# First loads of a gated mix kernel: x tile 0 split over two DMA queues by partitions, the other x tiles from SyncE, the Wk chunks but one from ScalarE

## The chip, the cores and the metric

One core of a Trainium2 chip runs the kernel. The metric is the device time of one execution in microseconds (us). Each kernel was run several times and profiled; a profile's times count from the first instruction of the span, which is about 2 us shorter than the device time. Engines are PE (TensorE's matmuls), PEld (its weight loads), DVE (VectorE), ACT (ScalarE), POOL (GpSimd) and SP (SyncE). SPq and ACTq are the instructions with which SyncE and ScalarE issue transfers on their DMA queues.

## The reference, cut to what matters

The output mixes two branches over one input x of 2048 x 512 elements in bf16: linear attention with 32 heads, and a layernorm with an MLP over tokens, gated by a sigmoid.

```python
qkv = x @ wqkv                         # D = 512, Wk is columns 512 to 1023
phi = lambda t: where(t > 0, t + 1, exp(t)) + 1e-6
kv  = einsum("bhsd,bhse->bhde", phi(k), v)
...
return g * a + (1 - g) * b
```

Only the start matters here: the first product is k = x @ Wk. It needs x transposed, tile by tile (a tile is 128 rows of x, 128 KB), and Wk in four chunks of 128 rows (128 KB each, `wk0` to `wk3`).

## The kernel before

The first eight loads go out on two queues in turn. The tiles x0 to x3 are transposed on PE; later tiles are transposed by the DMA. Six dummy matmuls on a constant (`warm_up`) keep PE busy until x0 lands.

```python
load_x(nc.sync, 0, 1)          # load_x(queue, first tile, tiles)
load_x(nc.scalar, 1, 1)
load_wk(nc.sync, 0)
load_x(nc.scalar, 2, 1)
load_x(nc.sync, 3, 1)
for k, q in ((1, nc.scalar), (2, nc.sync), (3, nc.scalar)):
    load_wk(q, k)
load_xT(4, 2)                  # DMA transposes, from SyncE
...
warm_up(6)
...
transpose_tile(0, False)       # four 128x128 transposes on PE, then a copy to xT
transpose_tile(1, True)
transpose_tile(2, False)
...
for k in range(2):             # six kacc matmuls: tiles 0 to 2, chunks wk0, wk1
    for t in range(HEADS - 1):
        k_part(t, (k,))
transpose_tile(HEADS - 1, True)
...
for t in range(HEADS):         # 14 kacc matmuls: the rest of tiles 0 to 3
    k_part(t, range(2 if t < HEADS - 1 else 0, ND))
    k_phi(t)
# ... (then kacc of tile t and gacc of tile t - 4 in turn, and all other stages)
```

PE takes its instructions in this order, so the transposes of x1 wait for x1 even when something later could run.

## Time and profile before

| | before |
|---|---|
| device time, median (lowest to highest of 4 runs) | 165.77 us (165.58 to 165.94) |
| span of the profiled run | 163.6 us |
| PE busy | 159.9 us, 98% |
| first `kacc` matmul starts | 4.82 us |
| first `gacc` matmul starts | 9.85 us |

These lines of the page of the kernel before give the span, each engine's busy time, PE's busy tenths in 40 slices, and the chain that ended last:

```profile
span 163.6 us, 2078 instructions
...
PE 159.9 (98%) x785; PEld 73.6 (45%) x785; DVE 87.8 (54%) x200; ACT 58.7 (36%) x90; POOL 18.3 (11%) x37
...
PE   7999999999999999999999999999999999999993
...
PE 98%; DVE 0%; issue 0%
```

PE is the limit from the first slice to the last, so a microsecond that PE loses anywhere is a microsecond of the kernel.

The chain view of the kernel before, for the first 14 us (start, duration, what):

```profile
0.84 2.72 PE wps L108 x6
3.56 1.47 PE pt L194 x12
5.03 1.74 PE kacc L108 x6
6.77 0.22 PE pt L194 x4
6.99 3.02 PE kacc L108 x14
10.01 0.86 PE gacc L108 x4
```

`wps` are the warm-ups, `pt` the transposes. Six warm-ups take 2.72 us, about 0.43 us each in steps of start to start. Fourteen later `kacc` matmuls of the same size take 3.02 us, 0.216 us each: PE starts at half speed. In the trace the steps change between 5.25 and 5.96 us.

The waits of the first 14 us, and the first two issues of SyncE in the timeline (start, duration):

```profile
PEld L194 <- DMA xs<-in_A_x_dram: 1.0, 2, 0.8
```

```profile
0.81 0.40 SPq L124 DMA_DIRECT2D xs<-in_A_x_dram  x1
1.27 0.41 SPq L127 DMA_DIRECT2D wk_sb<-in_A_wqkv_dram  x1
```

The weight loads of the transposes wait 1.0 us in two waits. The longer one, 0.75 us, passes while PE still works on the warm-ups.

### The profile page before, as it was taken

Reading aid. Unit: us, or ns where it says so; the run is one execution under the profiler, and the core shown is the slowest. Engines: PE = TensorE matmul, PEld = TensorE weight load, DVE = VectorE, ACT = ScalarE, POOL = GpSimd, SP = SyncE. Lnnn points to the kernel's source line nnn. Section 1 sums busy time; section 2 is a strip of 40 time slices with the busy share of each in tenths; the row PEclk is TensorE's granted clock in tenths of the full one; section 3 lists DMA queues with packets and bytes.
Section 4 is the critical chain, followed back from the end, with each engine's and each line's share of the span. In section 5 each row is a group of like instructions: output and inputs, shape, how many; then the busy total and the mean of one; then the engine's idle time right before and its main releaser. Section 6 shows DMA issues by size and latency. Waiting matters only on the chain.

```text
span 163.6 us, 2078 instructions
## 1 busy us (share of the span) xinstructions
PE 159.9 (98%) x785; PEld 73.6 (45%) x785; DVE 87.8 (54%) x200; ACT 58.7 (36%) x90; POOL 18.3 (11%) x37
## 2 busy tenths in 40 slices
PE   7999999999999999999999999999999999999993
PEld 3444444444544444434444444444444444444452
DVE  0599999958999999109995301156221111111112
ACT  3463386658478373311332113111112222211110
POOL 5000710200200000001055500050000000000000
DMA  5999999999930005800993499932010000111001
GB/s 152 242 243 236 294 300 344 349 348 348 317 78 0 0 0 188 264 0 0 277 303 109 149 289 307 337 126 98 32 36 32 32 32 32 42 50 41 32 32 32
DMA packets 30057, 25.05 MB, mean 153 GB/s; under 512 B 7968, under 2 KB 29472, under 8 KB 30048
## 3 DMA queue, kind: packets, MB, share of 16 engines
q1 hardware_dynamic: 28032, 22.02, 45.5%
q0 software_dynamic: 1440, 2.38, 5.4%
q10 hardware_dynamic: 576, 0.52, 1.1%
q8 instruction: 6, 0.10, 0.2%
q14 instruction: 3, 0.02, 0.0%
HBM read 21.11 MB, written 2.23 MB: 143 GB/s over the span
## 4 chain that ended last, share of the span: by engine, by line
PE 98%; DVE 0%; issue 0%
PE uacc L108 30%; PE yps L108 30%; PE kacc L108 9%; PE aps L108 8%; PE qacc L108 8%; PE gacc L108 8%; PE wps L108 2%; PE pt L194 1%; PE denps L108 1%; PE kvps L108 1%; DVE ot L474 0%; PE zps L108 0%; PE pt L323 0%
## 5 line engine op out<-in xcount | busy, mean ns | idle before, releaser
L108 PE MATMUL uacc<-hs,w1c 128*128 128x512 bf16 x224 | 52.1, 379 | 0.0
L108 PE MATMUL yps<-uT,w2c 128*128 128x512 bf16 (+2 forms) x238 | 51.0, 366 | 0.0
L474 DVE SCALAR_TENSOR_TENSOR ot<-yps,c,a_sc 128x512 bf16<-128x512 f32 (+2 forms) x17 | 12.2, 720 | 45.9 <-PE yps L108 45.8
L108 PEld LDWEIGHTS <-w2c 128*128 128x128 bf16 x238 | 22.8, 98 | 25.9
L108 PEld LDWEIGHTS <-w1c 128*128 128x128 bf16 x224 | 21.7, 98 | 26.0 <-issue 0.4
L461 ACT ACTIVATE a_sc<-aps,c,gg 128x512 f32<-128x512 f32 x16 | 12.4, 778 | 46.7 <-PE aps L108 43.0
L317 ACT ACTIVATE uT<-uacc,bcol 128x512 bf16<-128x512 f32 x14 | 9.3, 687 | 27.7 <-PE uacc L108 27.7
L108 PE MATMUL aps<-W2sb,pqT 128*128 128x512 bf16 x64 | 16.4, 379 | 0.0
L108 PE MATMUL qacc<-xT,wq_sb 128*128 128x512 bf16 x64 | 16.4, 379 | 0.0
L108 PE MATMUL kacc<-wk_sb,xT 128*128 128x512 bf16 x64 | 16.4, 385 | 0.0
L108 PE MATMUL gacc<-pk,xs 128*128 128x512 bf16 x64 | 15.8, 379 | 0.0
L244 ACT ACTIVATE hs<-xs,nmr,rstd 128x512 bf16<-128x512 bf16 x16 | 12.8, 805 | 1.9 <-DVE nmr L238 1.9
L204 ACT ACTIVATE e<-qacc 128x512 bf16<-128x512 f32 x16 | 9.6, 597 | 10.1 <-PE qacc L108 9.2
L413 POOL DMA_DIRECT2D rex<-rd_dram x16 | 9.5, 603 | 23.0 <-DVE pqT L415 18.2
L204 ACT ACTIVATE e<-kacc 128x512 bf16<-128x512 f32 x16 | 9.3, 595 | 6.9 <-PE kacc L108 6.8
L208 DVE SCALAR_TENSOR_TENSOR pk<-kacc,e 128x512 bf16<-128x512 f32 x16 | 11.1, 692 | 0.6
L208 DVE SCALAR_TENSOR_TENSOR pqT<-qacc,e 128x512 bf16<-128x512 f32 x16 | 11.1, 692 | 0.6
L228 DVE BATCH_NORM_STATS2 stats<-xs 128x6 f32<-128x512 bf16 x16 | 10.9, 682 | 0.0
L205 DVE TENSOR_SCALAR e<-e 128x512 bf16<-128x512 bf16 x32 | 9.0, 282 | 3.3 <-ACT e L204 3.3
L400 DVE CUSTOM_DVE_ANT_0 junk<-xs,gw_b 128x512 bf16<-128x512 bf16 x16 | 9.8, 685 | 0.0
L269 DVE TENSOR_TENSOR zacc<-zacc,pk 128x512 f32<-128x512 f32 x14 | 9.6, 686 | 0.2
L108 PEld LDWEIGHTS <-wq_sb 128*128 128x128 bf16 x64 | 6.3, 98 | 7.5
(64 smaller groups left out, 70.1 us busy)
## 6 DMA issues: line engine op xcount, KB each, us to landing
w2c<-in_B_w_dram SPq DMA_DIRECT2D x8, 896.0 KB, 7.5
w1c<-in_B_w_dram SPq DMA_DIRECT2D x2, 2048.0 KB, 15.5
w1c<-in_B_w_dram SPq DMA_DIRECT2D x3, 1024.0 KB, 12.3
rex<-rd_dram POOLq DMA_DIRECT2D x16, 128.0 KB, 2.9
out_dram<-ot SPq DMA_DIRECT2D x15, 128.0 KB, 1.7
xs<-in_A_x_dram SPq DMA_DIRECT2D x3, 512.0 KB, 4.5
wq_sb<-in_A_wqkv_dram SPq DMA_DIRECT2D x1, 512.0 KB, 6.8
wv_sb<-in_A_wqkv_dram SPq DMA_DIRECT2D x1, 512.0 KB, 12.3
```

Of the source, the lines that this page charges most:

```text
L108: nc.tensor.matmul(o, lhsT=lhsT, rhs=rhs, start=start, stop=stop, **kw)
L204: nc.scalar.activation(out=e[:], in_=acc[:], func=ACT.Exp)
L205: nc.vector.tensor_scalar(out=e[:], in0=e[:], scalar1=1.0, scalar2=PHI_EPS, op0=ALU.min, op1=ALU.add)
L208: nc.vector.scalar_tensor_tensor(out=dst, in0=acc[:], scalar=0.0, in1=e[:], op0=ALU.max, op1=ALU.add)
L228: nc.vector.bn_stats(out=stats[:], in_=xs[:, t, :])
L244: nc.scalar.activation(out=hs[:, t, :], in_=xs[:, t, :], func=ACT.Identity, scale=rstd[:, t : t + 1], bias=nmr[:, t : t + 1],)
L269: nc.vector.tensor_tensor(out=zacc[:], in0=first, in1=pk[:, t, :], op=ALU.add)
L317: nc.scalar.activation(out=uT[:, j, :], in_=acc[:], func=ACT.Gelu_apprx_tanh, bias=bcol[:, j : j + 1])
L400: nc.vector.tensor_tensor_reduce(out=junk[:], in0=xs[:, t, :], in1=gw_b[:], scale=1.0, scalar=0.0, op0=ALU.mult, op1=ALU.add, accum_out=gp ...
L413: nc.gpsimd.dma_start(out=rex[:], in_=src.unsqueeze(1).to_broadcast([8, HEAD, SC]))
L461: nc.scalar.activation(out=a_sc[:], in_=aps[:], func=ACT.Identity, scale=gg[:, t : t + 1], bias=c2[:, t : t + 1],)
L474: nc.vector.scalar_tensor_tensor(out=ot[:, :W], in0=yps[:, :W], scalar=c1[:, t : t + 1], in1=a_sc[:, cs], op0=ALU.mult, op1=ALU.add,)
```

## The change

The intent, as the code shows it: get x0 sooner by carrying half of it on each queue, take out the warm-up that is then not needed, and keep the x tiles on one queue and the Wk chunks (all but wk2) on the other. Merging the first w2 load's halves takes back the transfer that the split adds, so the later loads reuse the same completion semaphores.

```diff
-    load_x(nc.sync, 0, 1)
-    load_x(nc.scalar, 1, 1)
-    load_wk(nc.sync, 0)
-    load_x(nc.scalar, 2, 1)
+    for q, p in ((nc.sync, slice(0, P // 2)), (nc.scalar, slice(P // 2, P))):
+        q.dma_start(out=xs[p, 0, :], in_=x_view[p, 0, :])
+    load_x(nc.sync, 1, 1)
+    load_wk(nc.scalar, 0)
+    load_x(nc.sync, 2, 1)
+    load_wk(nc.scalar, 1)
     load_x(nc.sync, 3, 1)
-    for k, q in ((1, nc.scalar), (2, nc.sync), (3, nc.scalar)):
-        load_wk(q, k)
+    load_wk(nc.scalar, 3)
+    load_wk(nc.sync, 2)
...
-    warm_up(6)
+    warm_up(5)
...
-        for f0 in (0, NF // 2):
-            f1 = f0 + NF // 2
+        for f0, f1 in ((0, NF // 2), (NF // 2, NF)) if c else ((0, NF),):
```

## The prediction

> **What bounds the kernel now.** TensorE. The page gives PE 98% busy (159.9 of 163.6 us), and the chain of waits is 98% PE. The change touches only the first 7 us of it: six warm-up matmuls (2.72 us), twelve x-tile transposes (1.47), six `kacc` matmuls (1.74), four transposes, then `kacc` back to back. Here PE waits for data only twice: in the waits view the transposes' weight loads wait 1.0 us for x tiles (0.75 us before 3.41, behind the warm-ups, and 0.24 us before 4.42). The limits are the arrival of x tiles 0 to 2 and the slow clock: in the timeline matmuls start 0.42 us apart until about 5.7 us and 0.216 us after it.
>
> **What the change moves.** No arithmetic. One 0.43 us warm-up goes, one issue (about 0.42 us of a sequencer) comes on SyncE; merging the first w2 load's halves takes one back near 60 us, where PE never waits for it.
>
> Before, issue to landing was: x0 0.81 to 3.4, x1 0.80 to 3.5, wk0 1.27 to 4.2, x2 (second on ACT) to 4.4, x3 1.73 to 5.7, wk1 to 5.9, wk2 to 6.5, wk3 to 6.8. Both queues moved bytes at like rates (DMA view by window), 290 to 350 GB/s together. The Trainium skill, "DMA: Bandwidth & Descriptors", Rules for kernel authors, calls splitting a transfer into partition halves pointless, since both use the same 16 engines; the trace agrees that the queues share. What the split changes is order: both queues first carry half of x0, so x0 no longer competes with x1. From packets moved per window I estimate
>
> - x0: 3.4 -> 3.2 us (ACT's half decides; its first packets came about 0.25 us after SP's)
> - x1: 3.5 -> 3.7
> - x2: 4.4 -> 4.6 (third on SP, behind 64 + 128 KB, not second on ACT behind 128 KB)
> - wk0, wk1: near 4.0 and 5.4, before PE needs them
> - x3 6.0, wk3 6.3, wk2 6.7.
>
> wk2 is now the ninth load: the compiled order makes SyncE wait for x0's first half before issuing it, because eight completion semaphores are reused in turn; before, the first DMA transpose had that wait (0.9 us). Its issue goes from 2.2 to about 3.1 us, but the rings are still full then.
>
> **On the critical path.** Warm-ups end near 2.98; transposes 0 start near 3.2 instead of 3.42, but transposes 2 near 4.6 instead of 4.42, so `kacc` starts 0.2 us later; half of that is slow-clock time, so it costs about 0.1 us. If x2 lands as before, the gain is likewise halved: removing 0.43 us of slow-clock warm-up saves at most about 0.2 us. I predict 165.6 us, range 165.1 to 166.4; faster by over 2% 0.01, within 2% 0.97, slower 0.02.
>
> **What would show it.** x0's transposes start at 3.0 to 3.3 us; the wait ahead of x2's grows from 0.24 to 0.3 to 0.6; first `kacc` 4.8 to 5.2; the `kacc` block before transpose 3 ends at 6.5 to 7.0; after that all stages keep their lengths, shifted by a constant. No PE wait for wk1, wk2, wk3 or w2c.
>
> **What would make it wrong.** (1) The clock. The Trainium skill, "TensorE: Matmul & The Clock Gate", Part 1, says that full clock needs a busy window of about 3.4 us; the trace agrees with a slow start. The change leaves about 0.8 us of PE idle there instead of about 0.2; if this delays the fast clock by a window, it costs up to 1.7 us: about 167.3. I give that 10 to 15%. (2) wk2 landing after 7.0 us stalls PE at full clock. (3) x2 landing as early as before: 165.3.

## The result, and the profile after

| | before | after |
|---|---|---|
| device time, median (lowest to highest of 4 runs) | 165.77 us (165.58 to 165.94) | 168.56 us (168.07 to 168.72) |
| ratio | | 1.0163, 95% interval 1.0144 to 1.0183 |
| span of the profiled run | 163.6 us | 166.8 us |
| x0, x1, x2 landed | 3.37, 3.54, 4.38 us | 3.23, 4.90, 6.11 us |
| first `kacc` matmul starts | 4.82 us | 6.38 us |
| first `gacc` matmul starts | 9.85 us | 12.86 us |

A ratio is the mean time of one kernel's runs over the mean of the other's of the same rounds, so it is not quite the ratio of the medians quoted. Landing times are the trace's start of issue plus its time to landing. The kernel is 2.8 us slower, and the time lies outside the predicted range of 165.1 to 166.4.

The same lines of the page after the change, with one more: this page has a row of the granted clock (PEclk, in tenths), which the page before did not print.

```profile
span 166.8 us, 2064 instructions
...
PE 160.1 (96%) x770; PEld 73.6 (44%) x784; DVE 87.8 (53%) x200; ACT 59.0 (35%) x90; POOL 18.2 (11%) x37
...
PE   6599999999999999999999999999999999999992
...
PEclk9879999999999999999999999999999999999999
...
PE 94%; DMA 2%; SPq 1%; issue 1%; DVE 0%
```

PE's busy time is nearly the same, but the first two slices (8 us) have gaps, and the second and third slices have a lower clock (8 and 7). The chain view of the changed kernel for the first 14 us:

```profile
0.80 0.58 SPq L135
...
1.44 0.82 SPq L124
...
2.31 3.79 DMA xs<-in_A_x_dram
...
6.15 0.41 PE pt L196 x4
...
6.59 0.43 DVE xT L202
...
7.07 1.68 PE kacc L108 x4
8.74 0.43 PE pt L196 x4
9.17 3.86 PE kacc L108 x14
13.03 0.86 PE gacc L108 x4
```

Up to 6.1 us the chain no longer runs through PE but through SyncE's issues and the transfer of x2. Behind it the same 14 `kacc` matmuls take 3.86 us instead of 3.02. From `gacc` on everything is shifted: the first `gacc` block starts at 13.03 in this chain against 10.01, 3.02 us later, and the first `yps` block at 102.46 against 99.44, also 3.02. So 3.02 of the 3.2 us between the two profiled spans arose before 13 us.

The waits of the first 14 us of the changed kernel:

```profile
PEld L196 <- DMA xs<-in_A_x_dram: 3.3, 3, 1.3
...
PE pt L196 <- DMA xs<-in_A_x_dram: 2.0, 3, 1.0
```

PE itself now stands still for x tiles, 2.0 us in three waits; before, only its weight loads had to wait. The granted clock shows what that does. Two windows of the changed kernel (columns: stretch, its length, busy time of PE, PEld, DVE, ACT and POOL with instructions, granted clock, DMA share, GB/s):

```profile
3.90:7.32 3.42, 1.53 (x13) 0.70 (x13) 1.16 (x3) 1.17 (x3) 0.00 (x0) 1.00 1.08 282
7.32:10.73 3.41, 3.41 (x13) 1.49 (x12) 1.27 (x5) 1.19 (x2) 0.00 (x0) 0.50 1.08 242
```

The trace's record of the clock has exactly these edges: full from 3.90 to 7.32 us, half from 7.32 to 10.73, full from there on. The full clock came early in this run, fell on a stretch in which PE was busy for 1.53 of 3.42 us, and was taken away for the next 3.41 us, when the data was there.

Only one of the four runs of the changed kernel shows this loss. Half clock for 3.41 of 166.8 us gives a mean granted clock of 0.99, as the profiled run has it; the other three have 1.0, and took 168.07 to 168.62 us all the same. In the traces at hand the clock record begins only with the first full clock, so a full clock that came late would fit these three (the order run below has that form); but no trace of them is on record, and this is not shown.

This gives a first sum for the profiled runs. The first `kacc` starts 1.56 us later (6.38 against 4.82). From there to the first `gacc` it takes 6.48 instead of 5.03 us, 1.45 more: 0.25 us of it is a wait for x2's copy, the rest slow clock.

The issues on SyncE's queue in the changed kernel's timeline:

```profile
0.80 0.58 SPq L135 DMA_DIRECT2D xs<-in_A_x_dram  x1
1.44 0.82 SPq L124 DMA_DIRECT2D xs<-in_A_x_dram  x1
```

The issue of 64 partitions took 0.58 us, not 0.40, and the whole tile behind it 0.82, not 0.41. The DMA view from 2.75 to 3.25 us, before the change (q1 is SyncE's queue, q10 ScalarE's; packets, MB, share of the engines),

```profile
q1 hardware_dynamic: 117, 0.11, 69.5%
q10 hardware_dynamic: 87, 0.07, 42.6%
```

and after it:

```profile
q10 hardware_dynamic: 90, 0.09, 91.6%
q1 hardware_dynamic: 15, 0.01, 16.5%
```

SyncE's queue, which now carries x1 and x2, nearly ran dry at the time when it should have moved x1.

### The profile page after: what moved, and what is told of

Same layout as the page of the kernel before. It is cut to its first block, busy times and chain, and to the rows that moved or that the text cites. A ratio compares the mean times of both kernels' runs of the same rounds, so it can differ in the third digit from the quotient of the medians.

```text
span 166.8 us, 2064 instructions
## 1 busy us (share of the span) xinstructions
PE 160.1 (96%) x770; PEld 73.6 (44%) x784; DVE 87.8 (53%) x200; ACT 59.0 (35%) x90; POOL 18.2 (11%) x37
## 4 chain that ended last, share of the span: by engine, by line
PE 94%; DMA 2%; SPq 1%; issue 1%; DVE 0%
PE yps L108 29%; PE uacc L108 29%; PE kacc L108 9%; PE qacc L108 8%; PE aps L108 8%; PE gacc L108 8%; DMA xs<-in_A_x_dram 2%; PE denps L108 1%; PE kvps L108 1%; PE wps L108 1%; PE pt L196 1%; SPq L124 0%; SPq L135 0%; DVE xT L202 0%; DVE ot L475 0%
## 5 line engine op out<-in xcount | busy, mean ns | idle before, releaser
L108 PE MATMUL kacc<-wk_sb,xT 128*128 128x512 bf16 x64 | 17.6, 407 | 0.1
L108 PEld LDWEIGHTS <-xT 128*128 128x128 bf16 x64 | 6.5, 104 | 8.2 <-issue 1.4
```

Of the source, the lines that this page charges most:

```text
L108: nc.tensor.matmul(o, lhsT=lhsT, rhs=rhs, start=start, stop=stop, **kw)
```

## The experiments

Three questions stood after the result. Is the order of the loads or the split to blame? Is the loss the late data alone, or also the clock? And what decides when a tile lands? There were twelve runs, one of them a repetition; all gave correct results. "Before" in each group is the kernel before, run on the same chip in the same rounds. Landing times differ by up to 0.9 us between runs of the same loads (x2 came at 4.70 to 5.61 us in the three profiles with the partition split alone), so they are quoted run by run, each from its own profile.

### The order without the split

```diff
+    load_x(nc.sync, 0, 1)      # whole, from SyncE
+    load_x(nc.sync, 1, 1)
+    load_wk(nc.scalar, 0)      # and on as in the changed kernel; warm_up(5)
```

> The changed kernel without the split: x0 whole on SyncE, then x1, x2, x3, wk2 there, wk0, wk1, wk3 on ScalarE's queue, five warm-ups, w2 load as before. Theory Order (x1 and x2 come late because they stand in line behind x0 on one queue while wk chunks, which nobody needs yet, take half of the bandwidth): x1 lands at 4.2 to 4.9 us, x2 near 5.7 to 6.1, full clock after 9 us, time 168.0 to 168.6. Rival Split (the half-tile issues, 0.58 us instead of 0.40, and the slow issue behind them, 0.82 us, make everything late): every issue takes 0.40 to 0.45 us, x1 and x2 land by 4.0 and 5.0, time below 166.8.

Measured: 168.5 us (167.13 to 168.69; before 165.65), ratio 1.0158, interval 1.0112 to 1.0205. SyncE's issues took 0.40 to 0.43 us. x1 landed at 4.16 us, x2 at 5.79, and the record of the full clock starts at 9.44. The chain of this run:

```profile
1.73 4.06 DMA xs<-in_A_x_dram
...
5.84 0.61 PE pt L195 x4
6.45 2.56 PE kacc L108 x6
```

Six `kacc` matmuls in 2.56 us are all at half speed. What follows: the order alone, with five warm-ups, costs as much as the whole change within the intervals (one of its four runs took only 167.13). Theory Order stands for the sum; the split is not needed for it.

### The split without the order

```diff
-    load_x(nc.sync, 0, 1)
+    for q, p in ((nc.sync, slice(0, P // 2)), (nc.scalar, slice(P // 2, P))):
+        q.dma_start(out=xs[p, 0, :], in_=x_view[p, 0, :])
```

> The kernel before, with x0 alone split in two; the rest of the order, six warm-ups and the w2 load as before (x1 and x2 now second and third on ScalarE's queue). Theory Order: the split by itself costs x1 and x2 at most half a tile of queueing, x1 lands by 4.0 and x2 by 5.0; PE idles less than 0.8 us, full clock near 5.7 us, 165.6 to 166.2. Rival Split: issues of 0.55 us and more and a slow issue after each half, x1 not before 4.5, x2 not before 5.5, full clock after 9 us, 167.5 to 168.6.

Measured: 166.74 us (166.35 to 168.77), ratio 1.0107, interval 1.0033 to 1.0181. Both theories missed. x1 landed at 3.81, x2 at 5.27 and the clock was full from 4.76: the median lies between the two expectations. Because of the outlier the same kernel was run again:

> The partition split alone once more (same kernel as e2_split_only, on another chip or at another time), because its four runs ran from 166.35 to 168.77. x2 third on ScalarE's queue at 4.7 to 5.3 us. If the split alone costs about 1 us as the median said: median 166.4 to 167.0, with some runs above 167.5 where the clock came late. If it costs nothing and that median was chance: 165.6 to 166.1.

Measured: 166.5 us (166.23 to 168.07; before 165.8), ratio 1.006, interval 1.0026 to 1.0094; x2 landed at 5.61, later than I had expected. The split alone costs something near 0.6 to 1.1%. One caveat: in this kernel ScalarE issues five loads instead of four, and its function-table load starts at 3.48 us instead of 2.70; part of the cost may lie there, which was not tested.

### The split by columns

```diff
+    for q, c in ((nc.sync, slice(0, D // 2)), (nc.scalar, slice(D // 2, D))):
+        q.dma_start(out=xs[:, 0, c], in_=x_view[:, 0, c])
```

> The kernel before with x0 split over the two queues by columns (128 partitions times 256 elements each) instead of by partitions (64 times 512); the rest as in the kernel before, so it stands against the run with the partition split alone (issues 0.58 and 0.56 us, the next SyncE issue 0.82, x2's transposes at 5.32). Theory Form (a transfer of 64 partitions is slow to issue): both column halves issue in 0.40 to 0.46 us, the next SyncE issue too; x2's transposes start before 4.9; 165.6 to 166.2. Rival Queue (any second transfer ahead of x1 and x2 costs this, whatever its form): x2's transposes after 5.1, 166.4 to 167.0.

Measured: 166.55 us (166.34 to 168.24; before 165.89), ratio 1.0058, interval 1.0007 to 1.0109. The timeline has SyncE's issues as:

```profile
0.81 0.40 SPq L135 DMA_DIRECT2D xs<-in_A_x_dram  x1
1.27 0.43 SPq L127 DMA_DIRECT2D wk_sb<-in_A_wqkv_dram  x1
```

So it is the form of 64 partitions that issues slowly, not half a tile of bytes; that part of Theory Form is right. x2 landed at 4.75, and x0 at 2.97, 0.40 sooner than in the kernel before. But the six warm-ups kept PE until 3.36, so the early x0 was not used (columns with fewer warm-ups were not run), and the time did not come down to what I expected: here PE waited for wk1, which landed at 6.32 (behind three transfers on ScalarE's queue). In time the two kinds of split cannot be told apart. Why 64 partitions issue slowly stays open.

### The changed kernel with dummy matmuls in its gaps

```diff
-    warm_up(5)
+    warm_up(6)
     transpose_tile(0, False)
+    warm_up(3)
     transpose_tile(1, True)
+    warm_up(2)
```

> The changed kernel with six warm-ups and five more dummy matmuls (three after x0's transposes, two after x1's), so that PE has work while it waits for x1 and x2. Theory Clock (most of the loss is that the idle time kept the clock slow): full clock near 5.7 us again though x1 and x2 land as late as in the changed kernel; kacc then starts near 6.6 at full clock; 166.8 to 167.3. Rival Lateness alone (the clock comes up late for some other reason, or the loss is the wait itself): full clock still after 9 us, 168.3 or more.

Measured: 167.07 us (166.53 to 167.13), ratio 1.0082, interval 1.0054 to 1.0111, half of the change's loss. The same two windows as above, in this run:

```profile
3.90:7.32 3.42, 3.33 (x21) 1.56 (x19) 1.69 (x5) 1.18 (x3) 0.00 (x0) 1.00 1.09 288
7.32:10.73 3.41, 3.41 (x21) 1.68 (x19) 2.45 (x6) 2.66 (x5) 0.00 (x0) 1.00 1.26 239
```

More work for PE went with a faster kernel, and the clock, full from 4.75 us, stayed full. The time is what theory Clock expected. The profile was kinder than I had assumed, though: it is of the fastest of the four runs, and x2 landed at 5.33 us in it, not at 6.1, so this run by itself does not separate the two causes cleanly. The next one does.

### The order alone with dummy matmuls

```diff
     transpose_tile(1, True)
+    warm_up(3)                 # on the order without the split; warm_up(6) at the start
```

> The changed order without the split (the earlier run took 168.5, full clock from 9.4 us), now with six warm-ups and three dummy matmuls between x1's and x2's transposes, where PE waited 1.0 us. Theory Clock: the arrivals stay (x1 near 4.2, x2 near 5.8) but the clock is full by 6.5 and stays so, 166.5 to 167.2. Rival Lateness: the wait for x2 is the loss, 168.2 or more.

Measured: 167.18 us (167.13 to 167.37; before 165.89), ratio 1.0073, interval 1.0056 to 1.009, against 1.0158 without the dummies. x2 landed at 6.16 us, 0.37 later than in the profile without them, and still the kernel was faster. This chain answers to the one above:

```profile
1.75 4.41 DMA xs<-in_A_x_dram
...
6.21 0.41 PE pt L195 x4
...
7.12 1.04 PE kacc L108 x4
```

Four `kacc` matmuls in 1.04 us are at full speed; the clock was full from 3.66 us. So about half of the loss of the order goes away when PE has work in the gaps: that is the clock's part. The other half, some 0.7%, stays with the late data. The halves are rough, since the clock in this profile was full even earlier than in the kernel before (3.66 us against some time from 5.25 to 5.96).

### The split alone with dummy matmuls

```diff
     transpose_tile(1, True)
+    warm_up(2)                 # on the split without the order
```

> The partition split alone (earlier run 166.35 to 168.77, x2's transposes at 5.32), with two dummy matmuls between x1's and x2's transposes. If the run of 168.77 was one in which the clock came late or was lost, all four runs now lie within 166.0 to 166.9 and none is above 167.2. If not, a run above 168 comes up again with about the same chance (one in four per run), and the median stays at 166.7.

Measured: 167.17 us (166.21 to 167.95), ratio 1.007, interval 1.0027 to 1.0114. The expectation failed: the spread stayed, and no gain is seen. In the profiled run (166.21) the clock was full from 3.54. A spread of 1.7 us would fit a clock that comes anywhere within one window of 3.4 us at half price, but only one of these runs has a trace, so this is argued, not shown.

### Fewer warm-ups in the kernel before

```diff
-    warm_up(6)
+    warm_up(5)
```

> The kernel before with five warm-ups instead of six, nothing else. It leaves one idle gap of about 0.43 us before x0. If a gap of this size is harmless to the clock: full clock near 5.7 us, 165.6 to 165.9. If any gap in this stretch delays the clock by a window: full clock after 8 us, 167 or more.

Measured: 166.02 us (165.74 to 166.22; before 165.65), ratio 1.0025, interval 0.9999 to 1.0052; full clock from 6.05. A gap of 0.4 us is harmless or nearly so. Taking out all six:

```diff
-    warm_up(6)
+    warm_up(0)
```

> The kernel before with no warm-up matmuls at all; no transfer changes, and x0 lands at 3.4 us in any case, so no data comes later. PE only idles 2.5 us at the start. Theory Clock: the first window that is busy enough ends later, full clock between 6 and 9.5 us instead of 3.5 to 6.8, each us of that costs half: 166.6 to 168.0. If idle time as such costs nothing here: the time of before, 165.4 to 166.2.

Measured: 166.84 us (165.86 to 167.41; before 165.8), ratio 1.0059, interval 1.0029 to 1.0089; full clock from 6.57 us, after 12 transposes and the first four `kacc` matmuls. No transfer was changed, and idle time at the start costs about 1 us; the interval holds it apart from zero. That it costs this through the clock is likely but not shown: x0 landed at 3.69 in this profile, 0.3 later than in the kernel before, and only this one of the six runs, one of the fastest, has a trace.

### The merged w2 load

```diff
-        for f0 in (0, NF // 2):
-            f1 = f0 + NF // 2
+        for f0, f1 in ((0, NF // 2), (NF // 2, NF)) if c else ((0, NF),):
```

> The kernel before with only the first w2 load made one transfer of 1792 KB. PE never waits for w2 in the profiles of before and after, so every theory expects the time of before, 165.4 to 166.0. A rival that puts part of the loss on this part of the change expects 166.2 or more and a PE wait for w2 near 100 us.

Measured: 165.84 us (before 165.89), ratio 0.9988, interval 0.9966 to 1.001. This part of the change does nothing to the time.

### All first loads on one queue

```diff
-    load_x(nc.scalar, 1, 1)
+    load_x(nc.sync, 1, 1)
     load_wk(nc.sync, 0)
-    load_x(nc.scalar, 2, 1)
+    load_x(nc.sync, 2, 1)      # x3, wk1, wk2, wk3 behind it, from SyncE too
```

> All eight first loads from SyncE's queue, in the order x0, x1, wk0, x2, x3, wk1, wk2, wk3 of the kernel before; no split, six warm-ups. Theory Bytes ahead (a tile lands when the bytes issued before it on both queues have moved): x2 has 384 KB before it, as in the kernel before, and lands at 4.4 to 4.9 us (its issue starts at about 2.2); 165.7 to 166.5. Rival Place (a tile's place in its own queue decides: first 3.4, second 4.2, third 5.8, fourth 6.2 to 6.5 us, as seen on both queues): x1 lands at 4.2, wk0 at 5.7, x2 after 6.0; 168 or more.

Measured: 166.0 us (165.77 to 166.12; before 165.8), ratio 1.0016, interval 1.0 to 1.0031. x0 landed at 2.94 us, x1 at 3.38, wk0 at 3.98, x2 at 4.58, x3 at 5.40. A place in a queue alone does not decide: x2 was the fourth on its queue and landed 1.2 us before the x2 that was third on SyncE's queue in the order experiment. The DMA view has the time of x2 from issue to landing, in the order experiment and here:

```profile
xs<-in_A_x_dram SPq DMA_DIRECT2D x1, 128.0 KB, 4.1
...
xs<-in_A_x_dram SPq DMA_DIRECT2D x1, 128.0 KB, 2.4
```

What fits is the bytes issued ahead on both queues. With 384 KB ahead x2 came at 4.58; with 512 KB ahead a tile came at 5.40 (x3 here), 5.79 (x2 in the order experiment) and 5.70 (x3 in the kernel before), but at 4.93 in the columns run (x3). With 640 KB ahead x2 came at 6.16 (the order with dummies, where the issue of wk3 started before that of x2). It is a fit to single profiles, and no run varied the bytes alone. The runs with the split by partitions stand out: with 384 KB ahead their x2 came at 4.70, 5.27 and 5.61, the one with columns at 4.75. And a tile with nothing beside it on the other queue comes sooner: x0 at 2.94, without any split.

### The intent of the change on one queue

```diff
+    load_x(nc.sync, 0, 1)
+    load_x(nc.sync, 1, 1)
+    load_x(nc.sync, 2, 1)
+    load_wk(nc.sync, 0)        # x3, wk1, wk2, wk3 behind it; warm_up(5)
```

> The intent of the change without its cost: all eight first loads on SyncE's queue, in the order x0, x1, x2, wk0, x3, wk1, wk2, wk3, and five warm-ups, because x0 landed at 2.94 us when no other queue moved bytes beside it. Theory Bytes ahead: x0 lands near 2.9, x1 3.4, x2 4.0, wk0 4.6; kacc starts near 4.6 instead of 4.8, PE idles less than 0.5 us before it. The gain lies in slow-clock time and is halved: 165.4 to 165.8, at best 0.3 us under the kernel before. Rival Place in the queue: x2 (third) after 5.5, 167.5 or more.

Measured: 165.59 us (165.52 to 166.06; before 165.85), ratio 0.9999, interval 0.9981 to 1.0018. x0 landed at 2.82, x1 at 3.79, x2 at 4.15, wk0 at 4.49; the first `kacc` started at 4.66 us against 4.82. The arrivals are as expected but for x1, and x0 is 0.55 us sooner than in the kernel before, but the time is the same. No version was found that beats the kernel before.

## Why the prediction was wrong, point by point

**PE bounds the kernel, and only the first 7 us are touched.** Right. After the first `gacc` every stage is shifted by the same 3.02 us; PE never waited for w2, and merging its load did nothing.

**x0 at 3.2 us.** The number is right, 3.23, but not the reason, so that is partly luck: I had ScalarE's half decide, and it landed at 2.94; SyncE's half came last. wk2 was issued at 3.25 us, near the 3.1 that I had said, but not after a wait for x0: the issue of x3, held up by the slow issues ahead of it, ended at 3.20, and the waits view of SyncE's queue lists no wait for a DMA there.

**x1 at 3.7 and x2 at 4.6.** This is the step that failed, the largest mis-sized term of the sum. They landed at 4.90 and 6.11. Two things were missed.

- I read x2's landing from its place on SyncE's queue (behind 64 + 128 KB) and a packet count, with a constant time from last packet to landing. What fits the runs without slow issues, with the one exception named above, is the bytes ahead on both queues. In the changed order x0, x1, wk0 and wk1 are issued before x2, 512 KB, where it was at most 384 KB before. The profile before had the answer: x3 with 512 KB ahead of it landed at 5.7, and I wrote that number down without using it.
- I took every issue for 0.42 us. The half took 0.58 and the issue behind it 0.82, so x1's issue ended at 2.26 instead of about 1.7. In the changed kernel x1 landed 0.74 us later than in the run of the same order without the split (4.90 against 4.16), though the profile of the same loads with dummies has it at 4.51, so the slow issues cost x1 0.35 to 0.74. In the time this is hidden: the order alone gives 1.0158, both together 1.0163.

**First `kacc` 0.2 us later, at a cost of 0.1 us.** Wrong in consequence: 1.56 us later.

**The clock.** The mechanism was named, with the right size of up to 1.7 us, but given only 10 to 15%, because I reckoned with 0.8 us of idle PE instead of the 2 us and more that came. The form was different as well, in the profiled run at least: the full clock was not late but was granted at 3.90 us and lost again at 7.32. The Trainium skill, "TensorE: Matmul & The Clock Gate", Part 1, describes a free-running window of 3.4 us; this trace agrees, with edges 3.41 us apart. Filling the gaps took the ratio from 1.0163 to 1.0082, and in the order alone from 1.0158 to 1.0073. The second pair is the cleaner one, since x2 came no earlier in it. So of the loss roughly one half is clock (0.0085 of 165.8 us is 1.4 us) and the other half is late data.

**The split is pointless.** I quoted the Trainium skill, "DMA: Bandwidth & Descriptors", Rules for kernel authors, for this and yet booked 0.2 us for x0. The runs agree with the page: with the partition split alone x0 came at 3.21, 3.26 and 3.41 us in three profiles against 3.37, hardly sooner, while x1 and x2 came later in all three. The same page's section "Issuing engines are not separate DMA queues" says that several issuing engines save only the issue time; the run from one queue agrees, 166.0 against 165.8 us.

## What to carry to other kernels

When first loads are regrouped, add up for each tile the bytes issued before it on all queues, in the order of need, and read a landing time for that sum from the trace you have; the queue it sits on says little. A wait that opens in the first microseconds of a PE-bound kernel can be paid twice, once as idle time and once as half clock on the work behind it. If the wait can't be removed, cheap dummy matmuls in the gap can win back the second payment (they did in two of three trials here), but not the first.

## What the Trainium skill lacked or had wrong

- "DMA: Bandwidth & Descriptors", Rules for kernel authors: two transfers to partition halves are called pointless, as seen here, but their issue cost is missing. A transfer of 64 partitions took 0.58 us to issue on SyncE against 0.40 for 128 partitions, and the full tile behind it 0.82 against 0.41; the same half as 128 partitions by 256 columns took 0.40.
- "TensorE: Matmul & The Clock Gate", Part 1 and its section "HAM oscillation — how this bites in real kernels": the rule asks for no idle gap over about 3.4 us. Here the full clock was lost after a window of 3.42 us in which PE was busy for 1.53 us (45%); PE's longest wait of this stretch was 1.0 us. In the second run of the split alone PE waited 1.30 us in a window with 2.02 of 3.41 us busy (59%, ending at 7.43), and the full clock stayed. So in these traces the share of the window fits, and the longest single gap does not; no run varied the one without the other.
- The same page doesn't say which share counts. By the busy time that the profile gives, full clock came after windows with 79% (2.69 of 3.42 us, the split alone with dummies, ending at 3.54) and 80% (2.72 of 3.41, the order with dummies, ending at 3.66), and did not come after 71% (2.44 of 3.41, the merged w2 load, ending at 3.28) or 57% (1.94 of 3.42, the order alone, ending at 6.03); 45% lost it, and 59% and 67% (2.27 of 3.41, the order with dummies, ending at 7.07) kept it. PE's transposes have to be counted for this: in the kernel without warm-ups the window that brought the full clock (3.16 to 6.57) had 2.84 us busy, of which the `kacc` matmuls alone make 1.58 us (46%), less than the 71% that did not bring it. One run each; the windows without a clock record of their own are counted back in steps of 3.41 us.
- The same page calls the ramp less than 1% of a typical span and advises not to fit a count of slow matmuls. The part put down to the clock here, about 0.8%, lies within that figure; and yet it was about half of a loss of 1.6%.
- No page says that the windows view of the profile shows 1.00 where the trace holds no clock record: those of the kernel before, whose page has no row PEclk, show 1.00 from the beginning, while its matmuls started 0.42 us apart until some time between 5.25 and 5.96 us and 0.216 apart after it. The steps between matmuls have to be read.
